# The odd 64 rows of a query weight as whole rows on 64 partitions, loaded on eight DMA engines

## The chip, the cores and the metric

The kernel runs on one core of a Trainium2 chip. The metric is device time in microseconds (us) of one execution; the time before is 383.69 us, the median of 3 runs (383.65 to 383.76). The engines are named as in the profile: PE (matrix products), DVE (vector work), ACT (activations), POOL, and SP, which here only issues transfers. Transfers are carried out by 16 DMA engines.

## The reference

One decode step of a transformer block for a batch of 4 with one token each: layer norm, attention over a window of the last 4096 cached positions, output projection, residual, layer norm, a gated feed-forward part, residual.

```python
W = min(4096, max(256, Sk // 4))                       # 4096
q = (x @ wq).reshape(B, Sq, Hq, Dh)                    # x: layernorm, D = 576; wq: 576 x 4096
k = jnp.repeat(k_cache[:, :, Sk - W:, :], rep, axis=1) # 16 heads of keys for 32 of queries
v = jnp.repeat(v_cache[:, :, Sk - W:, :], rep, axis=1)
p = _softmax(jnp.einsum("bhqd,bhkd->bhqk", q, k) * (Dh ** -0.5), axis=-1)
h = x + einsum("bhqk,bhkd->bhqd", p, v).reshape(B, Sq, Hq * Dh) @ wo
gate = layernorm(h) @ W_gate;  up = layernorm(h) @ W_up     # 576 x 4608 each
h2 = h + (relu(gate) * up) @ W_down                         # 4608 x 576
```

All inputs are bf16. Of the caches 2 x 67 MB are read, of the weights 25.4 MB.

## The kernel before

The kernel is written for each engine by hand: five programs (`prog_sync`, `prog_pool`, `prog_act`, `prog_dve`, `prog_pe`), each a fixed order of instructions. A small helper class (`Sched`, lines 50 to 100) gives names to results and puts a semaphore wait in front of an instruction where its `deps` ask for one.

**Transfers.** All large loads go through one list, `transfers`, that SP issues in order (`prog_sync`, lines 267 to 272). An entry has a destination range in one large buffer, `pool`, and waits only for the instruction that last used that range. The order is: `wq`, then the caches, then `wo`, `W_gate` and `W_up`, and `W_down` in nine pieces that get smaller towards the end (`WD`, line 251). The caches come as 32 pieces of 2 MB of K and as many of V ("duos", two heads of one batch entry), four slots of each in `pool`, V five pieces behind K.

**The query.** The 576 features do not divide by 128. The first 512 rows of `wq` are loaded as two transfers of 256 rows, two rows to a partition (lines 228 to 230); the product uses rows 0, 2, 4... and 1, 3, 5... in turn (`feat`, line 260). The last 64 rows are the odd part. Before, they are loaded so that each row is cut in two halves, and half u of row r lies on partition 2r + u (line 231): 128 partitions with 4 KB each. The matching input must then stand on partition 2r for the first half of the heads and on 2r + 1 for the second. For that, PE spreads the 64 values `x4` to 128 partitions with a 0/1 matrix `dup` (`XDUP`, line 530), and DVE multiplies by two masks `par` to give `xn4` with 2 x 4 columns, of which every second partition is zero (`XN4`, lines 405 to 407). Sixteen matmuls with 8 columns (lines 538 to 543) then add the odd part for two heads each: one in the lower and one in the upper half of the heads.

**What follows.** The query goes from PSUM through DVE (`D_QT`), PE (`QREP`), DVE (`D_QR`) and ACT (`QZ`) into the matrix that the scores use. For each half of a K duo, DVE transposes 32 x 32 blocks (`tr`, line 416), PE makes scores (`qk`), and for every fourth duo DVE, POOL and ACT make maximum, exponential and transposed probabilities. PE multiplies these with V five duos later (`pv`). The feed-forward part treats its own odd 64 rows as `wq` was treated, with `HDUP` (line 616) and `HN4` (lines 502 to 504); that use of `dup` and `par` stays.

Of the kernel before, what the change touches and what calls it, by code (L numbers as in the profile page):

```python
# [7 lines left out]
ALU = mybir.AluOpType  # L8
AX = mybir.AxisListType
FP32 = mybir.dt.float32  # L10
BF16 = mybir.dt.bfloat16

B = 4
D = 576
H = 32
KVH = 16
DH = 128
# [13 lines left out]
DUO = 2 * WIN * DH // 128  # L31
NKS = 4
# [70 lines left out]
def bass_sequential_preLN__sliding_block_cached__glu_gated_reglu__decode_kernel(  # L103
# [12 lines left out]
    with ExitStack() as es:  # L116
        cnt = [0]

        def sb(name, shape, dt):
            return es.enter_context(nc.sbuf_tensor(name, shape, dt))  # L120

        pool = sb("pool", [128, (NKS + NVS) * DUO], BF16)
# [9 lines left out]
        xn_bf = sb("xn_bf", [B, D], BF16)  # L132
        st1 = sb("st1", [B, 16], FP32)
        xnT = sb("xnT", [128, 4, B], BF16)
        xn4 = sb("xn4", [128, 2, B], BF16)
        x4 = sb("x4", [64, B], BF16)
        dup = sb("dup", [64, 128], BF16)
        par = sb("par", [128, 2], FP32)
# [27 lines left out]
        hnT = sb("hnT", [128, DC, 32], BF16)  # L166
# [11 lines left out]
        pb = [sc[:, i * 512:(i + 1) * 512] for i in range(4)]  # L178
        pb += [es.enter_context(nc.psum_tensor(f"pb{i}", [128, 512], FP32))[:, :] for i in range(4, 8)]
        PVB, OB, QB, QR, TPB = 4, 6, 6, 3, 7  # L180
        OSB, WOB, STB, SUB, DNB = 0, 3, 2, 5, 4
# [10 lines left out]
        S = Sched()  # L192
# [3 lines left out]
        transfers = []  # L196
        at = {}

        def add(name, key, off, n, consumer, make):

            free = []
            for u in list(users):
                if u[0] < off + n and off < u[1]:
                    if u[2] not in free:
                        free.append(u[2])
                    if off <= u[0] and u[1] <= off + n:
                        users.remove(u)
            users.append((off, off + n, consumer))
            at[name] = off
            transfers.append((name, key, free, lambda e: make(e, pool[:, off:off + n])))  # L210

        def duo(cache, d):
            b, m = divmod(d, KVH // 2)
            return cache[b, 2 * m:2 * m + 2, SK - WIN:SK, :].rearrange("s (p t) d -> p s (t d)", p=64)
# [11 lines left out]
        HQ = H * DH  # L226

        for c in range(2):
            add(("wq", c), f"wq{c}", NKS * DUO + 2 * c * HQ, 2 * HQ, "QMM",
                lambda e, o, c=c: e.dma_start(out=o, in_=A_wq[c * 256:(c + 1) * 256, :].rearrange("(p u) n -> p (u n)", u=2)))  # L230
        add(("wq", 4), "wq4", NKS * DUO + 4 * HQ, HQ // 2, "QMM",
            lambda e, o: e.dma_start(out=o, in_=A_wq[512:576, :].rearrange("r (u n) -> (r u) n", u=2)))
        for m in range(NDUO + VLEAD):
            if m < NDUO:
                add_K(m)
# [2 lines left out]
        for g in range(NWO):  # L238
            add(("wo", g), f"wo{g}", g * ROW, ROW, "ATTN",
                lambda e, o, g=g: e.dma_start(out=o,  # L240
                                              in_=A_wo[g * 1024:(g + 1) * 1024, :].rearrange("(p e) n -> p (e n)", e=8)))
        for c in range(2):
            for k, (kind, W) in enumerate((("wg", B_W_gate), ("wu", B_W_up))):
                add((kind, c), f"{kind}{c}", GU0 + (4 * c + 2 * k) * ROW, 2 * F, None,
                    lambda e, o, c=c, W=W: e.dma_start(out=o, in_=W[c * 256:(c + 1) * 256, :].rearrange("(p u) n -> p (u n)", u=2)))
        for u, (kind, W) in enumerate((("wg", B_W_gate), ("wu", B_W_up))):
            add((kind, 4), f"{kind}4", GU0 + 8 * ROW + u * HALF, HALF, None,
                lambda e, o, W=W: e.dma_start(out=o, in_=W[512:576, :].rearrange("r (u n) -> (r u) n", u=2)))
# [3 lines left out]
        for k, (f0, f1) in enumerate(WD):  # L252
# [4 lines left out]
                                  out=wd_sb[:, g0:g1, j0 * D:(j0 + nj) * D],  # L257
                                  in_=B_W_down[g0 * 128 * JJ:g1 * 128 * JJ, :].rearrange("(g p j) n -> p g (j n)", p=128, j=JJ)[:, :, j0 * D:(j0 + nj) * D])))
# [4 lines left out]
        def land(name):  # L263
            return ("L",) + (name if isinstance(name, tuple) else (name,))
# [101 lines left out]
        def prog_dve(S):  # L366
            v = "vector"
            S.op(v, lambda e: e.tensor_scalar(out=st1[:, 2:3], in0=st1[:, 0:1], scalar1=1.0 / D, scalar2=None, op0=ALU.mult),
                 deps=["A_SUM"], name="D1")
            S.op(v, lambda e: e.tensor_tensor(out=st1[:, 7:8], in0=st1[:, 2:3], in1=st1[:, 2:3], op=ALU.mult), deps=["D1"], name="D2")  # L370
            S.op(v, lambda e: e.scalar_tensor_tensor(out=st1[:, 8:9], in0=st1[:, 1:2], scalar=1.0 / D, in1=st1[:, 7:8],
                                                     op0=ALU.mult, op1=ALU.subtract), deps=["A_SQ", "D2"], name="D3")
            S.op(v, lambda e: e.tensor_scalar(out=st1[:, 3:4], in0=st1[:, 8:9], scalar1=0.0, scalar2=None, op0=ALU.max),
                 deps=["D3"], name="D_VARC")
            for ce in range(4):
                S.op(v, lambda e, ce=ce: e.tensor_copy(
                    out=sel[:, ce, :, :],
                    in_=bass.AP(tensor=ident_b, offset=64 * (ce // 2) + ce % 2, ap=[[128, 128], [0, 4], [2, 32]])),
                    deps=["IDB"], name=f"SEL{ce}")
            S.op(v, lambda e: e.tensor_copy(out=dup[:, :].rearrange("p (r u) -> p r u", u=2),  # L380
                                            in_=bass.AP(tensor=ident_b, offset=0, ap=[[128, 64], [1, 64], [0, 2]])), name="DUP")
            S.op(v, lambda e: e.tensor_reduce(out=par[:, :], in_=ident_b[:, :].rearrange("p (r u) -> p u r", u=2), axis=AX.X, op=ALU.add),
                 name="PAR2")
            for x in range(2):
# [5 lines left out]
                 deps=["M0"], name="M1")  # L390
            S.op(v, lambda e: e.tensor_scalar(out=mask[:, 2, :], in0=mask[:, 0, :], scalar1=-2 * BIG, scalar2=BIG, op0=ALU.mult, op1=ALU.add),
                 name="M2")
            S.op(v, lambda e: e.tensor_reduce(out=mask8[:, :], in_=ident_b[:, :].rearrange("p (s k) -> p s k", s=8), axis=AX.X, op=ALU.add), name="MASK8")
            for u in range(2):
# [4 lines left out]
                                                     op0=ALU.mult, op1=ALU.mult), deps=["D5"], name="D_NMR")  # L399
            S.op(v, lambda e: e.tensor_copy(out=xnT[:, :, :], in_=tpv[:, 0:16].rearrange("p (c b) -> p c b", b=B)),  # L400
                 deps=["TP1"], name="D_XNT0")
            S.op(v, lambda e: e.tensor_copy(out=x4[:, :], in_=tpv[0:64, 16:20]), name="D_XNT")
            S.op(v, lambda e: e.tensor_copy(out=xT[:, 0:4, :], in_=tpv[:, 32:48].rearrange("p (c b) -> p c b", b=B)), name="D_XT0")
            S.op(v, lambda e: e.tensor_copy(out=xT[0:64, 4, :], in_=tpv[0:64, 48:52]), name="D_XT")
            for u in range(2):
                S.op(v, lambda e, u=u: e.tensor_scalar(out=xn4[:, u, :], in0=pb[STB][:, 0:B], scalar1=par[:, u:u + 1], scalar2=None, op0=ALU.mult),
                     deps=["XDUP", "PAR2"], name=f"XN4{u}")

            def tr(i):
                deps = [land(("K", i // 2))]  # L410
# [38 lines left out]
            for i in range(2 * NDUO):  # L449
                tr(i)  # L450
                if i == 0:
# [3 lines left out]
                                                    in_=bass.AP(tensor=ident_f, offset=0, ap=[[128, 128], [4, 4], [32, NB], [1, 4]])),  # L455
                         deps=["IDF"], name="SELT")
                n, pos = divmod(i, 2 * NB)
# [5 lines left out]
                if i >= 29 and (i - 29) % KVH == 0:  # L463
# [4 lines left out]
                                            in_=bass.AP(tensor=ident_b, offset=0, ap=[[128, 128], [1, 8], [0, 8], [8, 16]])),  # L468
                 deps=[("CMP", NBATCH - 1)], name="S8")
            for b in range(B):  # L470
                if 29 + KVH * b >= 2 * NDUO:
                    norm(b)
            S.op(v, lambda e: e.tensor_tensor(out=oM.rearrange("p (x s b) -> p x s b", s=8, b=B),
                                              in0=sc[:, 0:1024].rearrange("p (x s b) -> p x s b", s=8, b=B),
                                              in1=bass.AP(tensor=mask8, offset=0, ap=[[8, 128], [0, 32], [1, 8], [0, B]]), op=ALU.mult),
                 deps=["OSEL", "MASK8"], name="D_OM")
            S.op(v, lambda e: e.tensor_reduce(out=oS.rearrange("p (x b) -> p x b", b=B),  # L477
                                              in_=oM.rearrange("p (x s b) -> p x b s", s=8, b=B), axis=AX.X, op=ALU.add),
                 deps=["D_OM"], name="D_OS")
# [6 lines left out]
                 deps=["H2"], name="D_R")  # L486
# [5 lines left out]
                                                     op0=ALU.mult, op1=ALU.subtract), deps=["S3"], name="S4")  # L492
            S.op(v, lambda e: e.tensor_scalar(out=st2[:, 20:24], in0=st2[:, 16:20], scalar1=0.0, scalar2=EPS, op0=ALU.max, op1=ALU.add),
                 deps=["S4"], name="D_VARC2")
            S.op(v, lambda e: e.reciprocal(out=st2[:, 28:32], in_=st2[:, 24:28]), deps=["A_STD2"], name="S6")
            S.op(v, lambda e: e.scalar_tensor_tensor(out=st2[:, 32:36], in0=st2[:, 8:12], scalar=-1.0, in1=st2[:, 28:32],
                                                     op0=ALU.mult, op1=ALU.mult), deps=["S6"], name="S7")
# [3 lines left out]
            S.op(v, lambda e: e.tensor_tensor(out=hnT[:, :, 0:B], in0=tmp5[:, :, :], in1=nmr_bc, op=ALU.add), deps=["N1", "HN4Z"], name="N2")  # L501
            for u in range(2):
                S.op(v, lambda e, u=u: e.tensor_scalar(out=hn4[:, u, 0:B], in0=pb[SUB][:, 400:400 + B], scalar1=par[:, u:u + 1], scalar2=None, op0=ALU.mult),
                     deps=["HDUP"], name=f"HN4{u}")
            for x in PARTS[2:] + PARTS[:2]:

                S.op(v, lambda e, x=x: e.tensor_tensor(out=hh[:, x[0], :, x[1]:x[2]], in0=part(1, x, "j f"), in1=gate_sb[:, x[0], :, x[1]:x[2]], op=ALU.mult),  # L507
                     deps=[("GU", x[3]), ("RELU", x[0], x[1])], name=("HH", x[0], x[1]))
                if x[2] == 32:
                    S.op(v, lambda e, g=x[0]: e.transpose(out=hhT[:, g * JJ:(g + 1) * JJ, :].rearrange("p f b -> p (f b)"),  # L510
                                                          in_=hh[:, g, :, :].rearrange("p j f -> p (j f)")),
                         deps=[("HH", x[0], x[1])], name=("HHT", x[0]))
# [3 lines left out]
        def prog_pe(S):  # L516
            t = "tensor"

            def mm(o, l, r, start, stop, deps=(), name=None, skip=False):
                S.op(t, lambda e: e.matmul(o, lhsT=l, rhs=r, start=start, stop=stop, skip_group_check=skip),  # L520
                     deps=deps, name=name, signal=name is not None)

            for k, (src, base) in enumerate(((xn_bf, 0), (x_bf, 32))):
                for c in range(DC):
# [2 lines left out]
                    S.op(t, lambda e, c=c, w=w, src=src, base=base: e.transpose(  # L527
                        out=tpv[0:w, base + c * 4:base + (c + 1) * 4], in_=src[0:B, feat(c)], identity=ident_b[0:B, 0:B]),
                        deps=["A_XN", "IDB", land("x")] if k == 0 and c == 0 else [], name="TP1" if last else None, signal=last)
            mm(pb[STB][:, 0:B], dup[:, :], x4[:, :], True, True, deps=["D_XNT", "DUP"], name="XDUP")  # L530
            first = True
            for c in range(4):
                s = at[("wq", c // 2)] + (c % 2) * HQ
                for h in range(H):
                    mm(pb[QB][:, h * B:(h + 1) * B], pool[:, s + h * DH:s + (h + 1) * DH], xnT[:, c, :], first, False,
                       deps=[land(("wq", c // 2))] + (["D_XNT"] if first else []) if h == 0 else [], skip=True)
                    first = False
            s = at[("wq", 4)]
            for h in range(H // 2):
                o = pb[QB][:, 0:H * B].rearrange("p (u x) -> p u x", u=2)[:, :, h * B:(h + 1) * B]  # L540
                mm(o, pool[:, s + h * DH:s + (h + 1) * DH], xn4[:, :, :], False, h == H // 2 - 1,
                   deps=[land(("wq", 4)), "XN41"] if h == 0 else [],
                   name="QMM" if h == H // 2 - 1 else None, skip=True)
            for ce in range(4):
                mm(pb[QR][:, ce * 128:(ce + 1) * 128], sel[:, ce, :, :].rearrange("p g k -> p (g k)"), qT_sb[:, :], True, True,
                   deps=["D_QT", "SEL3"] if ce == 0 else [], name="QREP" if ce == 3 else None)
# [55 lines left out]
            for e_ in range(8):  # L602
                mm(sc[:, e_ * 128:(e_ + 1) * 128], S8[:, e_ * 128:(e_ + 1) * 128], oT_all[:, :, :].rearrange("p h b -> p (h b)"), True, True,
                   deps=[("NORM", b) for b in range(B)] + ["S8"] if e_ == 0 else [], name="OSEL" if e_ == 7 else None)
            for g in range(NWO):
                wv = pool[:, at[("wo", g)]:at[("wo", g)] + ROW].rearrange("p (e n) -> p e n", e=8)
                deps = [land(("wo", g))] + (["D_OX"] if g == 0 else [])
# [5 lines left out]
                           g == 0 and n == 0 and e_ == 0, last, deps=deps, name="ATTN" if last else None, skip=True)  # L613
                        deps = []
            mm(pb[SUB][:, 320:360], ones_f[:, :], R_sb[:, :, :, :], True, True, deps=["D_R"], name="STAT")
            mm(pb[SUB][:, 400:400 + B], dup[:, :], hnT[0:64, 4, 0:B], True, True, deps=["N2"], name="HDUP")

# [88 lines left out]
```

## Time and profile before

| | before |
|---|---|
| time, median of 3 runs | 383.69 us |
| profiled execution: span from first to last instruction | 382.2 us |
| busy PE / DVE / ACT / POOL | 287.7 / 206.5 / 53.5 / 8.2 us |
| moved by DMA | 159.84 MB, mean 418 GB/s |
| DMA queue of SP and of ACT (q1 and q10) | 12392 and 8 packets |
| instruction queues (q8 and q14) | 13 and 4 packets |

The span is that of one profiled execution; the median of the runs includes 1.49 us more, the start and the end of an execution outside the first and last instruction. The profile shows busy time per engine, the span in 40 slices with the busy tenths of each engine and of the DMA engines, the DMA queues, and a chain of waits: the work followed back from the last instruction, at each step to what released it. In it "DMA" is time in which the next step waited for data, "SPq" time between issues of transfers. A line such as `PE L520 MATMUL sc<-x,dup 64*128 64x4 bf16 x1` is a group of matmuls from line 520 (the helper `mm`, through which nearly all matmuls go) that writes tile `sc` from `x` and `dup`, with 64 x 128 weights and 4 columns; where a prediction or reading speaks of "x128", 128 such instructions were merged.

Besides, the trace holds each DMA packet (start, duration, size, queue; without the number of the engine that carried it) and each increment of a semaphore by a DMA engine.

### The profile page before, as it was taken

How to read it: one execution, taken by the hardware profiler on the slowest of the kernel's cores; microseconds unless marked ns; L12 is line 12 of the kernel's file. 1: busy time of each engine (PE TensorE's matmuls, PEld its weight loads, DVE VectorE, ACT ScalarE, POOL GpSimd, SP SyncE). 2: the span in 40 equal slices, each digit the busy share in tenths (PEclk: the TensorE clock that was granted, in tenths of full speed). 3: DMA queues.
4: the chain of work that ended last, by engine and by line, in shares of the span. 5: the costliest groups of instructions: out<-in, count | busy, mean ns of one | idle time of the engine just before them, and what ended most of it. 6: DMA issues, size and time to landing. Idle time of an engine off the chain costs nothing.

```text
span 382.2 us, 3916 instructions
## 1 busy us (share of the span) xinstructions
PE 287.7 (75%) x1697; PEld 124.5 (33%) x1712; DVE 206.5 (54%) x193; ACT 53.5 (14%) x129; POOL 8.2 (2%) x22
## 2 busy tenths in 40 slices
PE   0069749977997799669967996799589796956565
PEld 0053213322432243224322432243224233344331
DVE  0369789369437854774477548744865442042030
ACT  4021050021102110211021103010300021010020
POOL 4100000000000000000000000000000000000000
PEclk9999988997998799989998999899989996965677
DMA  8999999999999999999999999999999999999994
GB/s 307 434 424 422 436 422 429 431 425 427 426 429 430 424 429 430 425 429 429 429 425 430 425 427 432 424 430 427 427 430 425 427 431 424 419 430 424 420 416 198
DMA packets 12417, 159.84 MB, mean 418 GB/s; under 512 B 1384, under 2 KB 1520, under 8 KB 2672
## 3 DMA queue, kind: packets, MB, share of 16 engines
q1 hardware_dynamic: 12392, 159.59, 98.7%
q8 instruction: 13, 0.21, 0.2%
q14 instruction: 4, 0.03, 0.0%
q10 hardware_dynamic: 8, 0.00, 0.0%
HBM read 159.58 MB, written 0.00 MB: 418 GB/s over the span
## 4 chain that ended last, share of the span: by engine, by line
PE 50%; DVE 18%; issue 16%; ACT 6%; DMA 5%; SPq 3%; POOL 1%; POOLq 0%
PE sc L520 27%; PE pb L520 23%; DVE kT L416 6%; ACT P L344 5%; DMA pool<-in_B_W_down_dram 5%; DVE probT L435 4%; DVE rmx L419 4%; SPq L256 3%; POOL bcm L295 1%; DVE P L477 1%; DVE bias L431 0%; DVE rowsum L440 0%; DVE pmax L422 0%; DVE t L427 0%; DVE bmin L429 0%
## 5 line engine op out<-in xcount | busy, mean ns | idle before, releaser
L416 DVE STREAM_TRANSPOSE kT<-pool 128x2048 f32<-128x2048 f32 x64 | 144.5, 2291 | 54.4 <-DMA pool<-in_A_k_cache_dram 47.6
L520 PE MATMUL sc<-kT,qz 128*128 128x512 bf16 x497 | 133.1, 422 | 48.4 <-DVE kT L416 45.1
L520 PE MATMUL pb<-pool,prob 128*16 128x512 bf16 x512 | 118.5, 391 | 0.0
L520 PEld LDWEIGHTS sc<-kT,qz 128*128 128x128 bf16 x512 | 49.2, 102 | 128.6 <-DVE kT L416 53.2
L520 PEld LDWEIGHTS pb<-pool,prob 128*16 128x16 bf16 x512 | 44.0, 92 | 72.4 <-issue 19.0
L344 ACT ACTIVATE P<-sc,bias 128x512 f32<-128x512 f32 x32 | 22.2, 718 | 176.8 <-DVE bias L431 176.8
L419 DVE TENSOR_REDUCE rmx<-sc 128x2 f32<-128x2048 f32 x8 | 18.3, 2292 | 34.9 <-PE sc L520 34.9
L435 DVE STREAM_TRANSPOSE probT<-P 128x2048 f32<-128x2048 f32 x8 | 18.5, 2312 | 7.9 <-ACT P L344 7.9
L527 PE MATMUL pb<-ident_b,xn_bf 4*128 4x4 bf16 (+1 forms) x5 | 0.4, 175 | 19.6 <-ACT xn_bf L308 19.6
L329 ACT COPY cp<-pb 128x512 f32<-128x512 f32 x8 | 4.7, 585 | 67.9 <-PE pb L520 67.9
L520 PE MATMUL pb<-selT,cp 128*128 128x16 f32 x64 | 8.7, 269 | 4.4 <-ACT cp L329 4.4
L520 PEld LDWEIGHTS pb<-selT,cp 128*128 128x128 f32 x64 | 9.0, 208 | 6.5 <-ACT cp L329 5.4
L351 ACT CAST prob<-probT 128x1024 bf16<-128x1024 f32 x8 | 8.4, 1044 | 19.0 <-DVE rs L438 19.0
L444 DVE RECIPROCAL rs_sb<-pb 128x32 f32<-128x32 f32 x4 | 1.4, 339 | 17.8 <-PE pb L520 17.8
L507 DVE TENSOR_TENSOR P<-pb,P 128x288 bf16<-128x288 f32 (+1 forms) x2 | 0.8, 400 | 17.3 <-PE sc L520 17.3
L520 PE MATMUL pb<-pool,probT 128*4 128x288 bf16 x72 | 6.1, 310 | 5.4 <-DMA pool<-in_B_W_down_dram 5.4
L295 POOL PARTITION_ALL_REDUCE bcm<-pmax x8 | 3.1, 388 | 291.5 <-DVE pmax L422 291.5
L322 ACT COPY qz<-qrep 32x64 bf16<-32x64 bf16 x32 | 7.8, 244 | 7.3 <-DVE qrep L453 7.0
L520 PE MATMUL sc<-oX,pool 128*128 128x4 bf16 (+1 forms) x160 | 5.9, 172 | 3.7 <-DVE oX L480 3.7
L520 PE MATMUL pb<-pool,hnT 128*32 128x288 bf16 (+1 forms) x48 | 4.0, 405 | 6.0 <-DMA pool<-in_B_W_up_dram 6.0
L520 PE MATMUL sc<-pool,hnT 128*32 128x288 bf16 (+2 forms) x112 | 6.8, 366 | 0.6 <-DMA pool<-in_B_W_gate_dram 0.6
L520 PEld LDWEIGHTS sc<-oX,pool 128*128 128x128 bf16 (+1 forms) x160 | 5.8, 114 | 4.0 <-issue 3.9
(107 smaller groups left out, 80.1 us busy)
## 6 DMA issues: line engine op xcount, KB each, us to landing
pool<-in_A_k_cache_dram SPq DMA_DIRECT2D x32, 2048.0 KB, 27.9
pool<-in_A_v_cache_dram SPq DMA_DIRECT2D x32, 2048.0 KB, 25.9
pool<-in_A_wo_dram SPq DMA_DIRECT2D x4, 1152.0 KB, 21.7
pool<-in_B_W_gate_dram SPq DMA_DIRECT2D x2, 2304.0 KB, 24.8
pool<-in_B_W_up_dram SPq DMA_DIRECT2D x2, 2304.0 KB, 27.3
pool<-in_A_wq_dram SPq DMA_DIRECT2D x2, 2048.0 KB, 10.1
pool<-in_B_W_down_dram SPq DMA_DIRECT2D x2, 1296.0 KB, 24.1
pool<-in_B_W_down_dram SPq DMA_DIRECT2D x5, 432.0 KB, 25.8
```

Source lines behind the costliest of these rows:

```text
L256: lambda e, g0=g0, g1=g1, j0=j0, nj=nj: e.dma_start(out=wd_sb[:, g0:g1, j0 * D:(j0 + nj) * D], in_=B_W_down[g0 * 128 * JJ:g1 * 128 * JJ, : ...
L295: S.op(g, lambda e, n=n: e.partition_all_reduce(bcm[:, n % 2, :], pmax[:, n % 2, :], 128, bass_isa.ReduceOp.max), deps=deps, name=("PAR", n))
L322: S.op(a, lambda e, src=src, dst=dst: e.copy(out=dst, in_=src), deps=deps, name=("QZ", n) if g == 3 else None, signal=g == 3)
L329: S.op(a, lambda e: e.copy(out=cp[:, n % 2, :], in_=pb[PVB + n % 2]), deps=deps, name=("CP", n))
L344: S.op(a, lambda e, n=n, th=th, u=u: e.activation(out=P[:, th * 1024 + u:(th + 1) * 1024:2], in_=sc[:, th * 1024 + u:(th + 1) * 1024:2], f ...
L351: S.op(a, lambda e, n=n: e.copy(out=prob[:, n % 2, :, :, :], in_=probT[:, :, 0:NHB].rearrange("p t (r x) -> p r t x", x=4)), deps=deps, na ...
L416: S.op(v, lambda e: e.transpose(out=dst, in_=src), deps=deps, name=("TR", i))
L419: S.op(v, lambda e: e.tensor_reduce(out=rmx[:, n % 2, :], in_=sc[:, :].rearrange("p (x u) -> p u x", u=2), axis=AX.X, op=ALU.max), deps=[( ...
L435: S.op(v, lambda e: e.transpose(out=probT[:, :, :].rearrange("p t j -> p (t j)"), in_=P[:, :]), deps=[("EXP", n, 1)] + ([("CMP", n - 1)] i ...
L444: S.op(v, lambda e: e.reciprocal(out=rs_sb[:, b, :], in_=pb[OB][:, 64 + b * H:64 + (b + 1) * H]), deps=[("SUM", b)], name=("RS", b))
L477: S.op(v, lambda e: e.tensor_reduce(out=oS.rearrange("p (x b) -> p x b", b=B), in_=oM.rearrange("p (x s b) -> p x b s", s=8, b=B), axis=AX ...
L520: S.op(t, lambda e: e.matmul(o, lhsT=l, rhs=r, start=start, stop=stop, skip_group_check=skip), deps=deps, name=name, signal=name is not None)
```

## The change

The odd 64 rows lie as whole rows on partitions 0 to 63, 8 KB each. They come by two transfers of 32 rows (`wq4`, `wq5`), made by a new helper, `eight`. It writes the instruction out with a source of three dimensions whose slowest has size 8, and a destination of 32 partitions. The product takes `x4` as it is, with 64 rows of weights: 32 matmuls of 4 columns, one for each head. `XDUP`, `XN4` and the buffer `xn4` go. Two waits that these had brought along move to the feed-forward part's own users of `par` and `dup`, `HN4` and `HDUP`.

```diff
-        xn4 = sb("xn4", [128, 2, B], BF16)
...
+        def eight(e, out, in_):
+
+            rows, n = in_.shape
+            src = bass.AP(tensor=in_.tensor, offset=in_.offset, ap=[[rows // 8 * in_.ap[0][0], 8], [in_.ap[0][0], rows // 8], [1, n]])
+            dst = bass.AP(tensor=out.tensor, offset=out.offset, ap=[out.ap[0], [1, 1], [1, n]])
+            return e.add_instruction(mybir.InstDMACopy(name=nc.get_next_instruction_name(), ins=e.lower_ap_dma(src),
+                                                       outs=e.lower_ap_dma(dst), queue="qSPDynamicHW", mode="Copy"))
...
-        add(("wq", 4), "wq4", NKS * DUO + 4 * HQ, HQ // 2, "QMM",
-            lambda e, o: e.dma_start(out=o, in_=A_wq[512:576, :].rearrange("r (u n) -> (r u) n", u=2)))
+        add(("wq", 4), "wq4", NKS * DUO + 4 * HQ, HQ, "QMM", lambda e, o: eight(e, o[0:32, :], A_wq[512:544, :]))
+        transfers.append((("wq", 5), "wq5", [], lambda e: eight(e, pool[32:64, NKS * DUO + 4 * HQ:NKS * DUO + 5 * HQ], A_wq[544:576, :])))
...
-            for u in range(2):
-                S.op(v, lambda e, u=u: e.tensor_scalar(out=xn4[:, u, :], in0=pb[STB][:, 0:B], scalar1=par[:, u:u + 1], scalar2=None, op0=ALU.mult),
-                     deps=["XDUP", "PAR2"], name=f"XN4{u}")
...
-                     deps=["HDUP"], name=f"HN4{u}")
+                     deps=["HDUP", "PAR2"], name=f"HN4{u}")
...
-            mm(pb[STB][:, 0:B], dup[:, :], x4[:, :], True, True, deps=["D_XNT", "DUP"], name="XDUP")
...
-            for h in range(H // 2):
-                o = pb[QB][:, 0:H * B].rearrange("p (u x) -> p u x", u=2)[:, :, h * B:(h + 1) * B]
-                mm(o, pool[:, s + h * DH:s + (h + 1) * DH], xn4[:, :, :], False, h == H // 2 - 1,
-                   deps=[land(("wq", 4)), "XN41"] if h == 0 else [],
-                   name="QMM" if h == H // 2 - 1 else None, skip=True)
+            for h in range(H):
+                mm(pb[QB][:, h * B:(h + 1) * B], pool[0:64, s + h * DH:s + (h + 1) * DH], x4[:, :], False, h == H - 1,
+                   deps=[land(("wq", 4)), land(("wq", 5)), "D_XNT"] if h == 0 else [],
+                   name="QMM" if h == H - 1 else None, skip=True)
...
-            mm(pb[SUB][:, 400:400 + B], dup[:, :], hnT[0:64, 4, 0:B], True, True, deps=["N2"], name="HDUP")
+            mm(pb[SUB][:, 400:400 + B], dup[:, :], hnT[0:64, 4, 0:B], True, True, deps=["N2", "DUP"], name="HDUP")
```

## The prediction

> **What bounds the kernel now.** I read the page's busy rows and queues first: which resource has no slack.
>
> ```profile
> DMA  8999999999999999999999999999999999999994
> GB/s 307 434 424 422 436 422 429 431 425 427 426 429 430 424 429 430 425 429 429 429 425 430 425 427 432 424 430 427 427 430 425 427 431 424 419 430 424 420 416 198
> ...
> q1 hardware_dynamic: 12392, 159.59, 98.7%
> q8 instruction: 13, 0.21, 0.2%
> q14 instruction: 4, 0.03, 0.0%
> ```
>
> The 16 DMA engines are busy from the second slice to the last but one, at a level 416 to 436 GB/s, while PE has 75% and DVE 54% of the span. So bytes per engine set the time. Two small queues carry instructions; they matter below.
>
> Second, the chain of waits at its end, and the DMA view of the last 13 us (40 slices of 0.33 us):
>
> ```profile
> 349.87 4.06 SPq L256
> 353.96 4.77 SPq L256
> 358.78 19.51 DMA pool<-in_B_W_down_dram
> 378.33 1.62 PE pb L520 x12
> 379.98 0.45 DVE out_sb L513
> ```
>
> ```profile
> DMA  9998999899999999988765433320000000000000
> GB/s 404 415 383 362 383 436 436 351 415 404 436 415 401 440 386 443 362 355 340 291 259 206 188 145 145 121 92 28 0 0 0 0 0 0 11 4 0 0 0 0
> ```
>
> The end waits 19.51 us for W_down. But the DMA row does not stop at once: from slice 18 on (376 us) the engines fall idle one after another for 3.3 us. The kernel ends with its latest DMA engine, not with the mean one.
>
> Third, the trace's own records, below these views: each DMA packet with its time, and each semaphore increment that an engine makes when its share of a transfer is done (DMA clock minus 11.39 us is the span's time). A 128-row transfer makes 16 increments. Within one engine the next packet starts 4 ns before the former ends, so an engine can be followed through the run. Three readings:
> - Rows of 16 KB follow each other every 607 ns, rows of 4 KB every 155 ns, plus 6 ns per increment, on every engine alike.
> - The engines never wait for an issue. When SP issues a transfer, the least loaded engine still has at least 4.75 us queued (the fifth K, issued at 28.8 us), 11 to 27 us mostly. So lateness once gained stays to the end.
> - The 16 increments of the last transfer land, before the latest one, by 3.60, 3.44, 2.89, 2.72, 2.68, 2.37, 2.04, 1.91, 1.63, 1.63, 0.78, 0.39, 0.27, 0.08, 0.04 and 0 us. The latest lands at 379.36 and the last matmuls start at 379.40.
>
> What makes engines late is the instruction queues. Each 16 KB packet of q8 sets one engine back by 1.5 us, and they go round eight engines (packets one to eight hit eight different engines, the ninth hits the first again). Call these the **code eight**. At the end they are the engines at 0, 0.04, 0.08, 0.27, 0.39, 1.63, 1.63 and 2.04. The **other eight** are at 0.78, 1.91, 2.37, 2.68, 2.72, 2.89, 3.44 and 3.60; of these, the one at 0.78 was hit twice by 8 KB packets of q14 (at 67.6 and 314.5 us, 1.0 us each), and those at 1.91 and 2.37 once each (at 100.8 and 339.1 us, 0.7 and 0.6 us).
>
> **The change part by part.** Around the query:
>
> ```profile
> 20.63 0.18 PE L520 MATMUL sc<-x,dup 64*128 64x4 bf16 x1 [0.32 <-DVE x L402]
> ...
> 20.74 3.58 PE L520 MATMUL pb<-xnT,pool 128*128 128x4 bf16 x128
> 20.85 0.35 DVE L406 TENSOR_SCALAR xn<-sc,par 128x4 bf16<-128x4 f32 x2
> 21.12 2.30 DVE L416 STREAM_TRANSPOSE kT<-pool 128x2048 f32<-128x2048 f32 x1
> 24.18 0.57 PE L520 MATMUL pb<-xn,pool 128*128 128x8 bf16 x16
> 24.79 0.29 DVE L452 CAST qT_sb<-pb 128x128 bf16<-128x128 f32 x1 [1.37 <-PE pb L520]
> ```
>
> ```profile
> pool<-in_A_k_cache_dram SPq DMA_DIRECT2D x32, 2048.0 KB, 27.9
> ...
> pool<-in_A_wq_dram SPq DMA_DIRECT2D x1, 512.0 KB, 13.1
> ```
>
> - *PE.* XDUP goes: 0.11 us (20.63 to 20.74). The 16 matmuls of 0.57 us become 32 of the small form, 3.44 us / 128 = 27 ns each, 0.86 us. QMM ends 0.86 - 0.57 - 0.11 = 0.2 us later, and the first scores with it. Half the rows (64 for 128) could make a matmul cheaper or not: -0.4 to +0.2 us.
> - *DVE.* Both XN4 go, 0.35 us ahead of the first K transpose. That then waits for K 0, which lands at about 19.7 us now and up to 1.2 us later then.
> - *Waits moved.* PAR2 to HN4 and DUP to HDUP: both were done by 16.6 us and are asked for after 350 us. Nothing. Queued behind HDUP on PE are the gate and up matmuls, which do not wait.
> - *SP.* One more issue, 0.42 us, ahead of all K issues; the engines hold 11.9 us of work at that point.
> - All this is hidden by the queued transfers. If that cover of 4.75 us were gone it would cost 0.2 to 0.6 us. After the change the least loaded engines have 1.25 us less, 3.5 us, still positive.
> - *The load itself.* Landing of the wq rows moves from 14.8 to about 16 us; QMM asks for them at 24.2. Nothing there.
> - *Bytes per engine.* This is the part that reaches the end. Before, each of 16 engines moves 8 rows of 4 KB: 8 x 155 + 6 = 1.25 us. After, eight engines move 4 rows of 8 KB in each of two transfers. An 8 KB row is not in the stream; between 155 ns for 4 KB and 607 for 16 KB the line gives 306 ns. The 8 KB packets of q14 took 309 to 325 ns beside the stream and 307 to 342 ahead of it (the first three, from rest, 493 to 540); bounds for a row in the stream 300 to 342. So 8 x 306 + 12 = 2.46 us: **+1.21 us** on the eight engines used (+1.17 to +1.50), **-1.25 us** on the eight left out. The total is the same; who is last is not.
>
> So all hangs on which eight. If it is the other eight, the code eight end 1.25 us earlier, but the engine at 0.78 moves to 0.78 - 1.21 = -0.43, past the old latest. If it is the code eight, the latest is 1.21 us later.
>
> Which eight cannot be read off the trace by number. Two hints. The x transfer of 4 rows makes one increment at its issue (1.35 us) and four at 2.04 to 2.13 us, where 128 rows make 16: so a short outer dimension means few engines. And when the first wq transfer starts all 16 engines from rest, the other eight start on average 0.11 us before the code eight, which start roughly in the order in which code goes round them. If starts run upwards in number, the other eight are the lower half. I take that, as the likelier.
>
> [...]
>
> **Sum.** Span 382.20; last landing 379.36 + 0.43 = 379.79, and the 2.84 us after it unchanged: 382.63. The median of the runs is 383.69, 1.49 us over the span; 383.69 + 0.43 = **384.12 us**, +0.11%.
>
> **The rivals.**
> 1. *The code eight are the ones used* (or a mixture with one of their five latest). Place: the last landing of W_down; it decides as soon as one of the engines at 0 to 0.27 is loaded. Price +1.21: 384.90 (to 385.2). For: the starts differ by only 0.11 us within a spread of 0.42, so the half is weakly known; a mixed eight ends here too. Against: that order. [...]
> 2. *Faster.* The other eight are used, and the engine at 0.78 is not that late, because its q14 packets fall elsewhere or not in every run. Then the next of the eight is at 1.91 - 1.21 = 0.70 before the old latest: -0.70, 382.99; with the packet on that one gone too, the code eight at -1.25 are last: 382.44. For: the code moves by three DVE and some thirty PE instructions. Against: two packets on one engine hardly vanish by that.
> 3. *No effect.* The two transfers use different halves, or all 16: 4 x 306 + 6 = 1.23 us each for 1.25: 383.69. For: two separate transfers. Against: same form, same queue.
>
> [...]
>
> **How the numbers follow.** Forecast 0.39, rival 1 0.37, rival 2 0.18, rival 3 0.06. The forecast's own range is 383.9 to 384.5 (row cost 300 to 342 ns). The range 382.7 to 385.0 takes in rival 1 and the most of rival 2. I call 0.2% (0.77 us, 382.92 to 384.46) what a measurement of this kernel tells from no change. Faster: rival 2 without its -0.70 end, 0.15. Slower: rival 1 and the forecast's upper edge, 0.40. Same: 0.45.
>
> **What would show it.** The two transfers make 9 increments each, one at issue and eight later. If the forecast is right, one engine alone is last in the last transfer, some 1.1 us after the next, and the spread of its 16 increments stays near 3.7 us. If rival 1 is right, three are last together and the first of the 16 lands 6.1 us ahead of them. In the timeline, 32 matmuls of 27 ns end QMM at about 25.0 us, and DVE L406 is gone. Wrong would be: engines that run dry in the middle (DMA row under 9 ahead of the last slices), or an 8 KB row over 400 ns.

## The result and the profile after

The changed kernel takes 384.68 us (median of 10 runs, 384.22 to 385.12); the kernel before, run beside it, 383.73 us (10 runs, 383.61 to 384.16). The ratio is 1.0022 (95% interval 1.0014 to 1.003): 0.95 us slower, more than the 0.77 us that I called distinguishable. The profiled execution took 384.35 us, with a span of 382.5 us against 382.2; it is one of the quicker ones of its ten.

The page of the changed kernel, the same rows as before (slices, queues, and the shares of the chain of waits):

```profile
DMA  8999999999999999999999999999999999999994
GB/s 314 430 421 416 428 425 433 426 425 430 426 428 430 423 432 432 420 432 430 421 432 427 430 428 425 428 432 425 425 432 427 427 428 427 417 431 428 417 417 190
...
q1 hardware_dynamic: 12328, 159.59, 98.6%
q8 instruction: 13, 0.21, 0.2%
q14 instruction: 4, 0.03, 0.0%
...
DMA 45%; PE 27%; DVE 16%; issue 5%; SPq 4%; ACT 3%; POOL 0%; POOLq 0%
```

The bytes are the same; the 64 packets that are missing are 128 half rows that became 64 rows. The DMA row looks as before. What differs shows only in the DMA view of the last 13 us (40 slices of 0.33 us):

```profile
DMA  9989899999999999989877852100000000000000
GB/s 393 425 340 404 340 415 383 415 447 404 401 415 422 397 411 372 390 355 372 326 301 298 308 213 96 46 28 21 25 4 0 0 0 0 0 11 4 0 0 0
```

Before, this row ran out in steps (88765433320). Now its end falls from 8 to 0 within five slices (85210), since eleven engines end within 1 us of each other, and then 28, 21 and 25 GB/s are left for 1 us. The highest rate in the 40 slices of the page of before is 436 GB/s for 16 engines, 27 GB/s for each, so what is left is one engine. One engine alone is last. The end of the timeline says what waits for it:

```profile
378.89 0.53 PE L524 MATMUL pb<-pool,probT 128*4 128x288 bf16 x6 [0.50 <-DMA pool<-in_B_W_down_dram]
379.60 0.65 PE L524 MATMUL pb<-pool,probT 128*4 128x288 bf16 x6 [0.18 <-DMA pool<-in_B_W_down_dram]
379.96 0.08 PEld L524 LDWEIGHTS pb<-pool,probT 128*4 128x4 bf16 x2 [0.27 <-DMA pool<-in_B_W_down_dram]
380.29 0.39 ACT L370 CAST out_sb<-pb 4x288 bf16<-4x288 f32 x1 [9.89 <-PE pb L524]
...
380.83 0.30 SPq L277 DMA_DIRECT2D out_dram<-out_sb  x1
```

The last landing is at 379.92 us (379.36 before), and the last weights are loaded into PE at 379.96. The casts of the output come only 0.31 us later than before, and with them the end of the span. The same rows of the kernel before:

```profile
379.40 0.09 PEld L520 LDWEIGHTS pb<-pool,probT 128*4 128x4 bf16 x2 [0.26 <-DMA pool<-in_B_W_down_dram]
379.98 0.39 ACT L363 CAST out_sb<-pb 4x288 bf16<-4x288 f32 x1 [10.21 <-PE pb L520]
```

From the last weights to the casts before took 0.58 us, where the changed kernel takes 0.33. The granted TensorE clock between 379.3 and 380.3 us was 0.50 in this execution of the kernel before and 1.00 in that of the changed one. Of the 14 profiled executions, the six with 0.50 at this place have 0.57 to 0.58 us there and the eight with 1.00 have 0.33 to 0.34. So the two spans, 382.2 and 382.5 us, show only 0.3 of the 0.56 us by which the landing is later.

In the list of the last transfer's 16 increments the engines now land before the latest by 4.86, 3.95, 3.23, 2.96, 2.07, 1.95, 1.80, 1.75, 1.73, 1.68, 1.63, 1.51, 1.43, 1.42, 1.12 and 0 us. The latest is the engine that the 8 KB packets of q14 set back twice (by 0.96 us after 67.2 us and 0.97 us after 317.7 us).

The start of the stream and the query, in the timeline of the changed kernel:

```profile
1.64 1.97 SPq L216 DMA_DIRECT2D pool<-in_A_wq_dram  x2
...
20.62 2.29 DVE L420 STREAM_TRANSPOSE kT<-pool 128x2048 f32<-128x2048 f32 x1
...
20.69 3.55 PE L524 MATMUL pb<-xnT,pool 128*128 128x4 bf16 x128 [0.41 <-DVE xT L411]
...
24.17 1.01 PE L524 MATMUL pb<-x,pool 64*128 64x4 bf16 x32
25.22 0.29 DVE L456 CAST qT_sb<-pb 128x128 bf16<-128x128 f32 x1 [2.31 <-PE pb L524]
```

The two new issues take SP 1.97 us together (1.23 and 0.69 us and the gap between them), where the former one took 0.42. The 32 products take 1.01 us, and the query is ready at 25.22 us, 0.43 us later than before. `wq4` and `wq5` make nine increments each, one at the issue and eight between 13.8 and 14.4 and between 15.1 and 15.6 us: eight engines. All 64 rows of 8 KB took 309 ns but for a few (longest 458).

### The profile page after: what moved, and what is told of

Same layout as the page of the kernel before. It is cut to its first block, busy times and chain, and to the rows that moved or that the text cites. A ratio compares the mean times of both kernels' runs of the same rounds, so it can differ in the third digit from the quotient of the medians.

```text
span 382.5 us, 3961 instructions
## 1 busy us (share of the span) xinstructions
PE 292.1 (76%) x1727; PEld 125.4 (33%) x1727; DVE 205.9 (54%) x191; ACT 53.4 (14%) x129; POOL 8.2 (2%) x22
## 2 busy tenths in 40 slices
DMA packets 12353, 159.84 MB, mean 418 GB/s; under 512 B 1384, under 2 KB 1520, under 8 KB 2544
## 3 DMA queue, kind: packets, MB, share of 16 engines
q1 hardware_dynamic: 12328, 159.59, 98.6%
## 4 chain that ended last, share of the span: by engine, by line
DMA 45%; PE 27%; DVE 16%; issue 5%; SPq 4%; ACT 3%; POOL 0%; POOLq 0%
DMA pool<-in_A_k_cache_dram 36%; PE sc L524 14%; PE pb L524 13%; DVE kT L420 9%; DMA pool<-in_B_W_down_dram 5%; DMA pool<-in_A_v_cache_dram 4%; SPq L263 4%; ACT P L351 2%; DVE probT L439 2%; DVE rmx L423 2%; DVE P L481 1%; DVE P L477 0%; POOL bcm L302 0%; DVE sel L383 0%; ACT qz L329 0%
## 5 line engine op out<-in xcount | busy, mean ns | idle before, releaser
L524 PE MATMUL sc<-kT,qz 128*128 128x512 bf16 x512 | 136.7, 421 | 46.4 <-DVE kT L420 44.3
```

## The experiments

Twelve kernels ran, each timed in five rounds beside the kernel before. First the table, with the difference in us taken against the kernel before that was timed beside it, and the interval of the ratio; "last landing" is that of the profiled execution against 379.36 us.

| kernel | median us | difference | ratio, 95% | last landing |
|---|---|---|---|---|
| the change | 384.68 | +0.95 | 1.0014 to 1.003 | +0.56 |
| rows16 | 385.27 | +1.48 | 1.0027 to 1.0054 | +1.46 |
| halves8 | 387.88 | +4.09 | 1.0094 to 1.0122 | +3.87 |
| half8 | 385.29 | +1.50 | 1.0025 to 1.005 | +0.43 |
| four32 | 387.57 | +3.78 | 1.0084 to 1.0112 | +3.77 |
| load_only | 384.77 | +0.90 | 1.0012 to 1.003 | +0.77 |
| compute_only | 383.78 | -0.09 | 0.9992 to 1.001 | -0.10 |
| extra8_4k | 384.01 | +0.14 | 0.9997 to 1.0015 | +0.11 |
| extra8_8k | 384.80 | +0.93 | 1.0012 to 1.0031 | +0.28 |
| extra8_2x8k | 385.75 | +1.96 | 1.0039 to 1.0064 | +1.72 |
| extra4_8k | 384.30 | +0.51 | 1.0005 to 1.0023 | +0.35 |
| extra16_4k | 385.28 | +1.49 | 1.0026 to 1.0051 | +1.27 |
| before_again | 383.75 | -0.04 | 0.9989 to 1.0007 | -0.08 |

### The load or the products?

load_only keeps the change's two loads and goes back to the former products:

```diff
+        add(("wq", 4), "wq4", NKS * DUO + 4 * HQ, HQ, "QMM", lambda e, o: eight(e, o[0:32, :], A_wq[512:544, :]))
+        transfers.append((("wq", 5), "wq5", [], lambda e: eight(e, pool[32:64, ...], A_wq[544:576, :])))
...
-            s = at[("wq", 4)]
+            s = at[("wq", 0)]
```

> The change's two loads with the products of the kernel before (XDUP, XN4, sixteen products of 8 columns); these products read rows of the first part of wq in place of the odd 64, so the odd part of the query is not the reference's. Theory L (the load alone makes the difference): as the changed kernel, 384.3 to 384.9 us. Rival P (the products, 0.43 us later at the query, or the shifted start of the K transposes): as before, 383.7 us. Both in part: between the two.

compute_only is the other half: the load before, the change's products. Its second edit, against the changed kernel (the first puts the load of before back):

```diff
-                mm(pb[QB][:, h * B:(h + 1) * B], pool[0:64, s + h * DH:s + (h + 1) * DH], x4[:, :], False, h == H - 1,
+                mm(pb[QB][:, h * B:(h + 1) * B], pool[0:64, s + (h % 16) * DH:s + (h % 16 + 1) * DH], x4[:, :], False, h == H - 1,
```

> The load of the kernel before (half rows on 128 partitions) with the products of the change: 32 products of 4 columns from 64 partitions, without XDUP and XN4. They read the half rows that lie there, so the odd part of the query is not the reference's. Theory L: 383.7 to 383.8 us, as before, although the query is ready 0.2 to 0.5 us later. Rival P: 384.3 us or more. The 32 products take 0.9 to 1.0 us in both.

load_only is 0.90 us slower, like the change (0.95); compute_only is not slower (-0.09, interval -0.3 to +0.4 us). The timeline of compute_only shows the products of the change at full length:

```profile
20.41 2.29 DVE L412 STREAM_TRANSPOSE kT<-pool 128x2048 f32<-128x2048 f32 x1
20.48 3.55 PE L516 MATMUL pb<-xnT,pool 128*128 128x4 bf16 x128 [0.41 <-DVE xT L403]
23.97 1.01 PE L516 MATMUL pb<-x,pool 64*128 64x4 bf16 x32
25.02 0.29 DVE L448 CAST qT_sb<-pb 128x128 bf16<-128x128 f32 x1 [2.31 <-PE pb L516]
```

and that of load_only the former ones, with the query ready at 24.23 us, a microsecond earlier than in the changed kernel:

```profile
23.63 0.57 PE L528 MATMUL pb<-xn,pool 128*128 128x8 bf16 x16
24.23 0.29 DVE L460 CAST qT_sb<-pb 128x128 bf16<-128x128 f32 x1 [1.33 <-PE pb L528]
```

So nothing of the query's path reaches the end, in either direction, as far as the interval of compute_only tells (0.3 to 0.4 us to either side). The load alone makes a difference as large as the change's.

### How much work on the used engines, and what it costs

Here the kernel before keeps its own load and products, and gets one more load that nobody reads. A helper as the change's `eight`, with the number of engines as an argument, issues it after `wq4`, and QMM waits for it.

```diff
+        add(("ex", 0), "ex0", (NKS + 3) * DUO, HQ, "QMM",
+            lambda e, o: spread(e, o[0:32, 0:2048], A_wq[0:32, 0:2048], 8))
...
-                   deps=[land(("wq", 4)), "XN41"] if h == 0 else [],
+                   deps=[land(("wq", 4)), land(("ex", 0)), "XN41"] if h == 0 else [],
```

> The kernel before (its load and its products) plus one extra load of 32 rows of 4 KB to partitions 0 to 31 on the eight engines that the change uses; nobody reads the data, QMM only waits for it. It adds 4 x 155 + 6 = 0.63 us to each of these eight engines and nothing to the others. Theory L (the end is the one engine with the most work in all, here the one at 0.78 us before the latest): 0.78 - 0.63 = 0.15 us are left, so the time stays: 383.7 to 383.9 us, and in the last transfer's list that engine stands 0.0 to 0.3 us before the latest. Rival M (bytes moved in all set the time: 0.63 us on half of the engines): +0.31 us, 384.1. Rival Q (the used eight hold the latest engine): +0.63 us, 384.4.

The others differ in the size: `[0:32, 0:4096]` in extra8_8k; the same twice, to partitions 0 to 31 and 32 to 63, in extra8_2x8k; `[0:16, 0:4096]` over four engines in extra4_8k; and a plain transfer of 128 rows of 4 KB in extra16_4k.

> The same with rows of 8 KB: 4 x 309 + 6 = 1.24 us on each of the eight engines. Theory L: 1.24 - 0.78 = +0.46 us, 384.25 us, last alone by about 0.46 us. Rival M: +0.62 us, 384.4, with the list of the last transfer hardly changed in order. Rival Q: +1.24 us, 385.0. If L holds for the order but the end comes more than 0.3 us later than its sum, the engine's lateness in this kernel is not the 0.78 us that one profiled execution of the kernel before showed.

> The kernel before plus two extra loads of 32 rows of 8 KB, to partitions 0 to 31 and 32 to 63, as the change's two, with its own load of the odd rows kept: 2 x (4 x 309 + 6) = 2.48 us on each of the eight engines. QMM waits for the extra data and does not read it. Theory L (one engine with the most work, a fixed margin m, then one for one): with m = 0.3 us from the two extra loads before, +2.2 us, 386.05 us, last alone. With m = 0.78: +1.7 us, 385.55. Rival M (bytes in all): +1.24 us, 385.1.

> The kernel before plus one extra load of 16 rows of 8 KB to partitions 0 to 15, through four engines: 1.24 us on each of the four, nothing on the other twelve. If the engine that q14 hits twice is one of the four lowest: as with eight engines, 384.6 to 384.8 us. If it is not: no change, 383.8 to 383.9 us, since the other engines that are used end 1.9 us or more before the latest. Rival M: +0.31 us, 384.15, in both cases.

> The kernel before plus one extra load of 128 rows of 4 KB through all 16 engines: 8 x 159 + 6 = 1.28 us on every engine. All theories of work per engine: +1.28 us, 385.1 us, and the list of the last transfer as before. Theory I (the engines have idle time somewhere, so that added work is partly hidden): less than +1.0 us.

Measured: 0.63 us on eight engines cost 0.14 us, 1.24 cost 0.93, 2.48 cost 1.96, and 1.28 us on all sixteen 1.49. Rival M (bytes in all) is out: 2.48 us on half of the engines would be 1.24, and the interval is 1.5 to 2.5. The DMA view of extra8_2x8k from 370 us on (slices of 0.35 us) shows the same tail as the change, longer (27 GB/s for more than 1 us, one engine). That of extra16_4k shows the steps of the kernel before, shifted:

```profile
DMA  9999969999999999999887876310000000000000
GB/s 457 408 408 438 485 279 378 378 398 418 388 418 418 414 421 401 368 381 361 348 338 308 335 272 226 133 60 23 27 27 13 0 0 0 0 0 10 3 0 0
```

```profile
DMA  9898999999899999999988665333300000000000
GB/s 428 358 465 338 378 408 398 388 458 438 338 428 378 448 438 385 428 404 395 408 328 322 272 252 202 133 153 149 106 23 0 0 0 0 0 13 0 0 0 0
```

The first list of last increments has one engine alone by 1.27 us, at +1.72 us; the second has its five latest within 0.2 us (0.39 before), at +1.27. With a margin m between the used engine that ends latest and the latest of all, the time grows one for one once the added work passes m: the three doses give m = 0.63 - 0.14 = 0.49, 1.24 - 0.93 = 0.31 and 2.48 - 1.96 = 0.52 us, each uncertain by 0.3 to 0.5 us to either side. The dose of extra4_8k went to four engines alone; it cost 0.51 us, and in the trace the engine that q14 hits twice is one of the four and ends last by 0.28 us. So that engine is one of the four that this load uses; whether these are the lowest in number the trace does not show. I had written 384.6 to 384.8 us for that case, and it came out at 384.3; part of the reason is in the next section. The same 1.24 us on eight engines cost 0.93. The intervals of the two (+0.2 to +0.9 and +0.5 to +1.2 us) overlap, so the runs do not tell whether the other four used engines add something.

### Is the margin of 0.78 us a fixed number?

before_again is the kernel before, unchanged.

> The kernel before, unchanged, for a second profiled execution of it. Theory V (the 0.78 us by which one of the used engines ends before the latest is not a fixed number; packets at about 22 us lengthen on four engines by an amount that differs between executions): this engine ends 0.1 to 0.5 us before the latest, where the packets at about 22 us take 1.2 us or more, or near 0.8 us again where they take 1.0 to 1.2 us. Theory F (the 0.78 us is fixed, and the change costs 0.5 us somewhere else): 0.7 to 0.85 us again whatever those packets take. Time 383.7 to 383.9 us in both.

In this second profiled execution the q14 engine ends 0.52 us before the latest, and in compute_only, whose load is the same, 0.25 us. The 0.52 lies just above what I gave theory V (0.1 to 0.5), and F's 0.70 to 0.85 is missed in both. Following each engine from packet to packet shows where time is lost. At about 22 us, in the transfer K1, packets of four engines take 0.7 to 1.8 us in place of 0.61. The trace does not number the engines, so whether they are the same four each time is not seen; but the q14 engine is always one of them, in the kernels that use eight engines all four are among the eight, and in extra4_8k they are exactly the four used ones. How much it loses there differs:

```
                 work added   lost at 22 us   sum: -0.78 + work     measured landing of the
                 on it, us    by it, us       + (lost - 0.54)       q14 engine - 379.36, us
before              0            0.54            -0.78                 -0.78
before_again        0            0.79            -0.53                 -0.59
compute_only        0            1.06            -0.26                 -0.34
extra8_4k           0.63         0.34            -0.35                 +0.05
extra4_8k           1.24         0.44            +0.36                 +0.35
extra8_8k           1.24         0.60            +0.52                 +0.28
the change          1.21         0.56            +0.45                 +0.56
load_only           1.21         1.03            +0.92                 +0.77
extra8_2x8k         2.48         0.63            +1.79                 +1.72
```

The third column adds nothing but the work and this loss to the place that the engine had in the first profile. In seven of the eight further rows it comes within 0.25 us. Without the loss seven of the eight would come within 0.34 us, so this step alone is a modest gain, and in extra8_8k it makes the sum worse. In extra8_4k the extra rows themselves were slow on that engine: three of the four took 184, 342 and 286 ns for 159, and the 16 KB row after them 0.71 us for 0.61, together 0.44 us, which is what the sum misses there. If every lengthened packet of that engine between 3 and 30 us is counted, 0.77 us in the first profile and 0.52 to 1.07 in the others, the sums come within 0.2 us in all eight rows. So the law of the prediction holds (each engine ends when its own work is done), and its input, the place of one engine, moves by half a microsecond between executions. Theory V fits how the margin moves; it does not say where the loss at 22 us comes from. In rows16, half8, halves8 and four32 no packet of 16 KB takes over 0.64 us at 20 to 25 us, and I found no transfer or instruction that goes with it. That stays open.

### Other ways to load whole rows

These ran first. rows16 asks for the whole rows by one plain transfer, costed on all 16 engines:

```diff
-        add(("wq", 4), "wq4", ..., lambda e, o: eight(e, o[0:32, :], A_wq[512:544, :]))
-        transfers.append((("wq", 5), "wq5", [], lambda e: eight(e, pool[32:64, ...], A_wq[544:576, :])))
+        add(("wq", 4), "wq4", NKS * DUO + 4 * HQ, HQ, "QMM", lambda e, o: e.dma_start(out=o[0:64, :], in_=A_wq[512:576, :]))
```

> The 64 rows lie whole on partitions 0 to 63 as in the changed kernel, with the same 32 matmuls, but come by one plain transfer on 16 engines: 4 rows of 8 KB each, 4 x 306 + 6 = 1.23 us per engine for 1.25 before. Theory L (the end is set by the DMA engine that finishes last, so only the share of each engine counts): the time of before, 383.73 us, within 0.2 us; the spread of the last transfer's 16 increments stays near 3.6 us with several engines within 0.4 us of the last. Rival P (the query part itself, 0.45 us later on PE, is what costs): 384.5 us or more, as the changed kernel.

halves8 is the kernel before with its 128 half rows written for eight engines:

```diff
-            lambda e, o: e.dma_start(out=o, in_=A_wq[512:576, :].rearrange("r (u n) -> (r u) n", u=2)))
+            lambda e, o: spread(e, o, A_wq[512:576, :].rearrange("r (u n) -> (r u) n", u=2), 8))
```

> The kernel before with one edit: the transfer of the half rows (128 partitions, 4 KB each) is written with a slowest source dimension of 8, so that eight engines carry 16 rows of 4 KB each: 16 x 155 + 6 = 2.49 us on these, nothing on the others. XDUP, XN4 and the matmuls are those of before. Theory L: as the changed kernel, 384.2 to 384.9 us, and one engine alone is last by about 1.1 us. Rival P: 383.73 us within 0.2.

half8 and four32 are the changed kernel with the first 32 rows written for 16 engines, and the other 32 for eight or for four:

```diff
-        add(("wq", 4), "wq4", ..., lambda e, o: eight(e, o[0:32, :], A_wq[512:544, :]))
+        add(("wq", 4), "wq4", ..., lambda e, o: spread(e, o[0:32, :], A_wq[512:544, :], 16))
-        ... eight(e, pool[32:64, ...], A_wq[544:576, :])))
+        ... spread(e, pool[32:64, ...], A_wq[544:576, :], 8)))
```

> The changed kernel with half the shift: 32 of the 64 rows by a plain transfer on 16 engines (2 rows each), 32 by one on eight engines (4 rows each). The lower eight carry 6 rows, 1.84 us, +0.59 against before; the others 0.61 us, -0.63. Theory L, with the lateness of before (-0.78 for the latest of the lower eight, 0 for the others): the last is -0.19, 383.5 us (383.3 to 383.8), below half of the way. A rival in which the cost grows in proportion to the shift: half of +0.95, 384.2 us.

> As the last one, but the second 32 rows go on four engines (8 rows each). These carry 10 rows, 3.06 us, +1.81 against before; the other twelve -0.63. Where the latest of the lower eight (0.78 before the last, the one that two packets of q14 had set back) sits decides: if it is not among the four lowest, the next latest of the lower eight can be there at most, -1.91 + 1.81 = -0.10: 383.6 us. If it is among the four: -0.78 + 1.81 = +1.03, 384.8 us. If the kernel ended with the mean of the engines: 383.73.

All four missed, by 1.5 to 4 us. The sums had taken one price for a row, however a transfer shares its rows out. The traces: 8 KB rows took 309 ns (median) in the change and in every extra load of 8 KB rows, but 618 in rows16, 459 in half8 and 509 in four32; the 4 KB rows of halves8 took 354 for 159. The 16 KB rows of K0 beside them took up to 1.27 us (rows16), 1.65 (halves8), 1.28 (four32) and 1.31 (half8) for 0.61. The first K transpose shows it, of rows16 and then of halves8:

```profile
20.99 2.31 DVE L411 STREAM_TRANSPOSE kT<-pool 128x2048 f32<-128x2048 f32 x1 [0.52 <-DMA pool<-in_A_k_cache_dram]
```

```profile
24.32 2.31 DVE L424 STREAM_TRANSPOSE kT<-pool 128x2048 f32<-128x2048 f32 x1 [3.08 <-DMA pool<-in_A_k_cache_dram]
```

In both it waits for K0, which it does not in the change. The trace does not name a packet's engine or partition, so why rows are slow in these forms and not in the change's is not shown. The form of a transfer by itself does not tell: the second load of half8 is written like the change's, and the rows of its two loads together have the median 459. With the measured row in place of the forecast one, the sum for rows16 becomes an estimate that fits: 4 rows x 618 ns = 2.47 us on each of 16 engines, where before each had 1.25 us: +1.22 us on all sixteen; its last landing is +1.46, with a spread of 3.4 us as before. For half8 I have no such account: its profiled execution (384.44 us) is far below its median of 385.29.

No version beat the kernel before. The part of this change that could is the relief of the unused engines. The q14 engine ends 0.25 to 0.78 us before the latest, so moving work d from the unused to the used engines should gain d until the two meet. That is an estimate of at most half of that margin, 0.1 to 0.4 us, and no run tests it.

## Why the prediction was right in kind and short in size

- *Where the time is decided.* Right. The end is the last landing of W_down, PE follows 0.04 us later, and work on PE, DVE and SP before it is hidden. compute_only and load_only show this apart. What comes after the landing is not fixed, as the sum had it (2.84 us): it took 2.61 us in the changed kernel, where the last matmuls had the granted clock 1.00 in place of 0.50. And the 1.49 us between span and median put one slower execution's span beside the median; in every execution that has both, the time is 1.74 to 1.88 us above the span. Neither enters the forecast of +0.43.
- *PE and DVE.* The 32 products took 1.01 us, not 0.86 (27 ns each), and the query came 0.43 us later, not 0.2. Hidden, as forecast. The first K transpose did start earlier, at 20.62 for 21.12 us; K0 had landed at 20.49.
- *SP.* 1.97 us for the two new issues, where the sum had one more of 0.42. Hidden: they end at 3.61 us, and the two transfers of `wq` issued ahead of them land from 7.7 us and up to 13.4 us.
- *Bytes per engine.* 309 ns for a row against 306 forecast; 2.46 us per engine. Right, but by luck: the price had no term for how a transfer shares its rows out, and 8 KB rows took 309 ns in both of the change's transfers. The first four experiments, costed with the same price, all missed: 459 to 618 ns for 8 KB, and 354 for 4 KB.
- *Which eight.* For the engine that matters, right: it is one of the used eight, and ends alone, the next one 1.12 us earlier (forecast 1.1). The choice, and with it the -0.78 + 1.21 of the sum and the lower eight and four lowest of half8 and four32, rested on the assumption that such a transfer goes to the lower half in number; no run shows that, since the trace does not number the engines. What the runs show in its place is eight increments for the outer dimension of 8 (the change), four for that of 4 (extra4_8k), and the same q14 engine in both. The picture of two separate halves was not quite right. Of the eight engines that q8 goes round, two are among the used ones: in the trace of the changed kernel the seventh and eighth packet hit used engines, in load_only the fifth and sixth, in extra8_8k the sixth and seventh, and two engines that are not used are never hit. Where the round starts differs. In the changed kernel the shared two are hit once each and stay 1.4 us behind; in load_only one of them is hit twice and ends 0.12 us before the latest. That is the mixture that rival 1 named, and it costs next to nothing in that execution.
- *The size.* The forecast was +0.43, measured +0.95 (interval +0.5 to +1.15), more than twice as much. The term that was mis-sized is the margin of 0.78 us: it was read from one execution, and two others with the same load give 0.52 and 0.25 us. With these three the sum is 0.43, 0.69 and 0.96; with their mean, 0.52, it is 0.69, inside the interval. The measured 384.68 lies outside the forecast's own 383.9 to 384.5, and inside the wide range only because that was stretched for rival 1: luck. "Same", the likeliest of the three outcomes with 0.45, is out by the threshold that the prediction set. (The 383.9 to 384.5 do not follow from the row cost either: 300 to 342 ns give 384.08 to 384.41.) The profiled execution of the change itself had a loss at 22 us of 0.56, almost that of the first profile, and there the last landing came +0.56 us, near the forecast; the run took 384.35. The median is 0.33 us above it. Those other executions left no packets to look at. That they lost more at 22 us, or had a shared engine hit twice, fits the wider spread (0.9 us over ten runs, for 0.55 before), but is argued; a granted clock of 0.50 at the last matmuls, worth 0.25 us above, could also have part in it.
- *The cover.* Forecast: the engines never wait for an issue, with 3.5 us left after the change. Wrong in one place. SP issues the fifth K (K4) at 29.25 us, its packets come about 2.9 us later, and by then seven of the unused engines, which are 2 to 3 us ahead, have run dry: gaps of 0.03 to 1.27 us between 32.1 and 33.3 us, three of them under 0.1. They cost nothing in this execution, because those engines end 1.5 us or more before the last one. They take away part of the relief that the unused engines got. The profiled executions of load_only and of the extra loads on four or eight engines have no such gap.
- *Rivals.* No effect and faster are out by the interval. Rival 1's time, 384.90, is nearer to the median than the forecast's 384.12; its mechanism (three engines last together, the first 6.1 us ahead) is not what the trace shows. Its other form, a mixed eight, is what the trace shows, but with the shared engines not last in the two profiled executions of this load.

## What to carry to other kernels

In this kernel, whose DMA engines hardly rest (98.6% in q1), the sum of bytes alone did not set the end: the change moves the same 159.84 MB, and its last landing came 0.56 us later, on one engine that ended 1.12 us after the next. So write down the landing of every engine in the last transfer and ask whose work an edit changes. A margin of a few tenths read from one execution is not a number to build on (0.78, 0.52 and 0.25 us in three with the same load): profile the kernel before more than once. And price a row from a run of the transfer as it will be written: the same 64 rows of 8 KB took 309 ns each (median) in the change and 618 in rows16.

## What I had not expected of the hardware

- Four engines lose 0.2 to 1.2 us each at about 22 us in nine of the profiled executions, always with the q14 engine among them. In extra16_4k two engines lose 0.2 to 0.3 us a little earlier, and in rows16, half8, halves8 and four32, whose loads of the odd rows were slow, none does. The cause is open.
- Instruction packets set the end of a kernel whose instruction traffic is 0.2% of the DMA time. A 16 KB packet of q8 takes 1.0 to 1.1 us and sets its engine back by 1.5 us, and 13 of them go round eight engines. It reaches the end here: the five engines hit twice land last in the kernel before, within 0.39 us of each other.
- The time that an issue holds SP is not fixed by its form. The two issues written out with three dimensions held it for 1.23 and 0.69 us in the change, the plain one that they replace for 0.42 in the kernel before; but the same plain issue, ahead of an extra load, held it for 1.09 us in extra8_4k and 0.43 in extra8_2x8k. What sets it is open.
